# Reworking the first four pairs of an attention-and-MLP kernel, and where pairs 4 to 7 stand

## The chip, the core and the metric

The kernel runs on one core of a Trainium2 chip. The metric is device time in microseconds for one execution. A core has five engines with instruction streams of their own: TensorE (PE; its weight loads are listed as PEld), VectorE (DVE), ScalarE (ACT), GpSimd (POOL) and SyncE (SP). Each works through its stream in order and waits on semaphores. SP here only issues transfers; ACT and POOL issue some of theirs too (in the profile SPq, ACTq, POOLq). Matrix products go to PSUM, which has eight banks of 128 x 512 f32.

## The reference, cut to what matters

```python
# q, k, v: (8, 8, 576, 64), s: (8, 8, 576)
scores = scale * np.matmul(q, k.transpose(0, 1, 3, 2))
s_pos = np.maximum(s, 0.0)
cum = np.cumsum(s_pos, axis=-1)
bias = -(cum[:, :, :, None] - cum[:, :, None, :])
scores = np.where(causal, -1000000000.0, scores + np.minimum(bias, 0.0))
scores = scores - np.max(scores, axis=-1, keepdims=True)
attn = np.exp(scores)
attn = attn / (np.sum(attn, axis=-1, keepdims=True) + 1e-09)
attn_out = np.matmul(attn, v)
x = attn_out.transpose(0, 2, 1, 3).reshape(4608, 512)
h = x @ w_in                          # w_in (512, 2048)
g = h * np.clip(h + 3.0, 0.0, 6.0) / 6.0
out = g @ w_out                       # w_out (2048, 512)
```

## The kernel before, in words

**Units.** There are 64 heads of 576 tokens, handled as 32 pairs. The 4,608 tokens go through the two layers in nine blocks of 512. Four pairs of one batch make up the 512 columns of x for its 576 tokens, so block 0 needs pairs 0 to 3.

**A pair p**, in the order of its tasks:

- `load_qk` (line 136) and `load_v` (146) bring q, k and v from DRAM as f32 through SP's queue, into three buffers in turn (`qkf`, bufs 3, and slot p % 3 of `v_f`). A row of a transfer is the 64 numbers of one token, 256 bytes. Token `t*128 + p` of the pair's 1,152 lies on partition p, column t.
- `load_aug` (159) brings four bias rows per pair, the sums of s split into three f16 parts (`kaug`) and one negated row (`qaug`), from DRAM scratch, where lines 469 and 472 have put them. Together with constant mask rows on partitions 68 to 127 (`mask_rows`, 125, copies from the tile `amask`) they are extra contraction rows of qT and kT, so that the bias comes out of the same product as the scores. For pair 0 the bias rows are copied on the chip (461 to 468).
- `cast_qk` (165) makes q and k f16 on POOL; `cast_v` (226) does it for v, on DVE for pairs 1 to 4 and on POOL otherwise.
- `transpose_group` (242) transposes 128 x 128 tiles on PE with an identity, in two groups (five and four tiles), each into one PSUM bank; DVE copies each group's q and k half to `qT` and `kT` (253).
- `scores_bank` (272) does a head's causal scores in four banks (`BANKS`, 259): products into one of three `S` banks, the exponential on ACT into `Pm` (290), and the triangular mask on POOL (295).
- `attend` (320) multiplies by v with a column of ones, so that the row sums come out too; after the second head of a pair, DVE does reciprocal and product (341, 343) into `xs`. There is one `O` tile of two banks, so the next pair's attend waits for that product.
- `x_transpose` (356) brings `xs` into `xT` through PE and a DVE copy (377), or from pair 8 on by a transposing transfer on SP's queue for three of four pairs. From pair 10 on q and k are transposed by such a transfer too (`cast_columns`, `transpose_dma`), which needs `decay_columns` (179), `load_columns` and `copy_columns` once.

**The layers.** `m1(n, f)` (403) is one of 16 column groups of the first layer of block n: four products of 128 x 512, relu on ACT (416), product on DVE (417) into `gT`. `m2(n, t4, part)` (421) is four products of the second layer; four parts make one 128 x 512 output, which DVE scales (439) and SP stores (441). `load_w_in(h)` and `load_w_out(c)` (382, 388) load the weights on POOL's queue, casting f32 to f16 in the transfer.

**PSUM.** Tag `M` has two banks (`bank`, 53; `half_bank`, 231, for early transposes), `S` three, `O` two, `Y` one.

**The order.** The schedule is written out by hand: what the Python code calls first stands first on each engine. `att_tasks(p)` (482) lists a pair's tasks with costs; `weave` (546) mixes such a list with a list of layer tasks in proportion to the costs, and `merged` (571) mixes the first layer of one block with the second layer of the block before. Before the loop come `keep_warm(18)`, pair 0's cast and transposes and `keep_warm(12)` (584 to 591; products of zeros). Then pairs 0 to 3 and pair 4's scores run alone (592). Block 0's first layer and eight of the sixteen parts of its second layer are woven with the rest of pair 4 and pairs 5 to 8 (602), block 1 with pairs 8 to 12 (603), and so on. In a pair's tasks, the second head of a pair is attended in the pair after it (`late`), and x is transposed there too (`back`).

**Weights.** w_in(0) and w_in(1) are issued by POOL in the tasks of pairs 1 and 2 (479), w_out in four pieces within m1(0) (598).

**Completion semaphores.** The program gives the transfers of SP's and ACT's queues eight semaphores in turn; a transfer waits at its queue's head until the eighth before it is complete.

Of the kernel before, what the change touches and what calls it, by code (L numbers as in the profile page):

```python
# [16 lines left out]
def kernel(  # L17
# [10 lines left out]
    nc = tc.nc  # L28
# [18 lines left out]
    NS = 3  # L47

# [3 lines left out]

    def bank():
        return psum.tile([128, 512], F32, tag="M", bufs=2, name="bank")
# [8 lines left out]
    amask_dram = nc.inline_tensor(amask_np, name="amask")  # L63
# [31 lines left out]
    amask = work.tile([128, 2, SEQ], F16, tag="amask", bufs=1)  # L95
    s_sb = work.tile([NH, SEQ], F32, tag="s0", bufs=1)
    nc.sync.dma_start(out=s_sb, in_=s.rearrange("b h t -> (b h) t"))
    nc.scalar.dma_start(out=amask[64:128], in_=amask_dram.ap().rearrange("i p t -> p i t"))
    nc.scalar.dma_start(out=ident, in_=ident_dram.ap())

# [18 lines left out]
    nc.gpsimd.memset(warm, 0.0)  # L119
    nc.gpsimd.memset(kT[:, :, W2:W2 + 64], 0.0)  # L120
    nc.gpsimd.memset(v_f[64:128, :, :, 4, :], 0.0)
    nc.gpsimd.memset(v_h[:, :, :, :, D:VW], 1.0)
    nc.gpsimd.memset(Pm[:, :, 1600:PW], 1.0)

    def mask_rows(sl, copy):
        for i, dst in enumerate((kT, qT)):
            copy(
                out=dst[64:128, sl, 0:W2].rearrange("p (h t) -> p h t", h=2),
                in_=amask[64:128, i:i + 1, :].to_broadcast([64, 2, SEQ]),
            )  # L130
# [5 lines left out]
    def load_qk(p, eng):  # L136
        b, h0 = (2 * p) // H, (2 * p) % H
        t = work.tile([128, NTR, 2, D], F32, tag="qkf", bufs=3, name=f"qkf{p}")
        for i, src in enumerate((q, k)):
            rows = src[b, h0:h0 + 2].rearrange("h s d -> (h s) d")  # L140
            eng.dma_start(  # L141
                out=t[:, :, i, :], in_=rows.rearrange("(t p) d -> p t d", p=128)
            )
        qk_f[p] = t

    def load_v(p, eng):
        b, h0 = (2 * p) // H, (2 * p) % H
        sl = p % NS
        for hh in range(2):
            eng.dma_start(  # L150
                out=v_f[:, sl, hh, 0:4, :],
# [3 lines left out]
            out=v_f[0:64, sl, :, 4, :],  # L155
# [9 lines left out]
    def cast_qk(p):  # L165
        t = work.tile([128, NTR, 2, D], F16, tag="qkh", bufs=2)
        nc.gpsimd.tensor_copy(out=t, in_=qk_f.pop(p))  # L167
        qk_h[p] = t

    xaug = cpool.tile([128, 2 * NTR, 64], F16, tag="c_xaug")  # L170
# [55 lines left out]
    def cast_v(p):  # L226
        sl = p % NS
        copy = nc.vector.tensor_copy if p in (1, 2, 3, 4) else nc.gpsimd.tensor_copy
        copy(out=v_h[:, sl, :, :, 0:D], in_=v_f[:, sl])  # L229

    def half_bank(early):

        if early:
            return psum.tile([128, 640], F16, tag="M", bufs=2, name="pTm")
# [7 lines left out]
    def transpose_group(p, g):  # L242
        t0, t1 = ((0, 5), (5, 9))[g]
        n = (t1 - t0) * 128
        pT = half_bank(p < 5)
# [10 lines left out]


# [4 lines left out]
        (896, [(1, 256, 576), (4, 512, 576)]),  # L262
# [379 lines left out]
```

## Time and profile before

| | us |
|---|---|
| median of 3 runs | 382.33 (381.08 to 383.68) |
| the profiled execution | 379.86 |
| its span, first to last instruction | 378.1 |
| PE, ACT, DVE, POOL busy in it | 353.6, 210.4, 190.8, 146.4 |
| first scores (L282) | 12.59 |
| first scores of pairs 1, 2, 3, 4 | 16.62, 24.92, 29.86, 36.64 |
| first m1(0) product (L408) | 42.78 |
| first m2(0) product (L430) | 73.16 |
| first m1(1) product | 88.70 |

Times inside the span count from its first instruction. A line of a group gives the source line, engine, operation, output and input tiles, count, then busy time and mean ns. A line of the waits gives who waited for whom, the total, the number and the longest. In a line of stretches the PEclk column is the granted TensorE clock as a share of full speed, and the DMA column the mean busy share of 16 engines, which can exceed 1 where packets of two queues overlap. `q1` is SP's queue, `q10` ACT's and `q0` POOL's.

### The profile page before, as it was taken

How to read it: one execution, taken by the hardware profiler on the slowest of the kernel's cores; microseconds unless marked ns; L12 is line 12 of the kernel's file. 1: busy time of each engine (PE TensorE's matmuls, PEld its weight loads, DVE VectorE, ACT ScalarE, POOL GpSimd, SP SyncE). 2: the span in 40 equal slices, each digit the busy share in tenths (PEclk: the TensorE clock that was granted, in tenths of full speed). 3: DMA queues.
4: the chain of work that ended last, by engine and by line, in shares of the span. 5: the costliest groups of instructions: out<-in, count | busy, mean ns of one | idle time of the engine just before them, and what ended most of it. 6: DMA issues, size and time to landing. Idle time of an engine off the chain costs nothing.

```text
span 378.1 us, 7609 instructions
## 1 busy us (share of the span) xinstructions
PE 353.6 (94%) x2780; PEld 219.8 (58%) x2780; DVE 190.8 (50%) x329; ACT 210.4 (56%) x406; POOL 146.4 (39%) x375
## 2 busy tenths in 40 slices
PE   7766778899999999999999999999999999999995
PEld 3454455566666666666666666666666655555542
DVE  5554466875545444544444445445444554454531
ACT  4745466456866666666656666666666543443310
POOL 4365444364565444444444554454453100000000
PEclk9989699999999999999999999999999999999999
DMA  8699999945999999999999998999854001010011
GB/s 181 137 204 193 194 208 249 210 105 132 200 186 243 204 211 200 216 203 203 197 190 199 214 208 179 206 211 200 185 114 106 31 30 55 28 55 29 28 66 74
DMA packets 184621, 59.38 MB, mean 157 GB/s; under 512 B 177828, under 2 KB 178212, under 8 KB 184584
## 3 DMA queue, kind: packets, MB, share of 16 engines
q1 hardware_dynamic: 182536, 54.52, 68.2%
q0 software_dynamic: 1632, 4.19, 5.9%
q8 instruction: 22, 0.36, 0.4%
q10 hardware_dynamic: 416, 0.19, 0.2%
q14 instruction: 15, 0.12, 0.1%
HBM read 37.41 MB, written 9.73 MB: 125 GB/s over the span
## 4 chain that ended last, share of the span: by engine, by line
PE 82%; DMA 9%; DVE 3%; ACT 2%; SPq 1%; issue 1%; POOL 1%; POOLq 0%; ACTq 0%; DVEq 0%
PE bank L408 31%; PE po L430 30%; PE S L282 9%; PE O L331 7%; DMA qkf<-in_k_dram 5%; DMA v_f<-in_v_dram 3%; PE bank L430 3%; ACT Pm L290 2%; PE pT L369 1%; DMA s_sb<-in_s_dram 1%; PE bank L450 1%; SPq L141 1%; POOL t L167 1%; DVE qkT L253 1%; DVE kaug L115 0%
## 5 line engine op out<-in xcount | busy, mean ns | idle before, releaser
L416 ACT ACTIVATE trl<-bank,bias 128x512 f32<-128x512 f32 x144 | 99.5, 691 | 111.8 <-PE bank L408 110.8
L417 DVE SCALAR_TENSOR_TENSOR gT<-trl,bank 128x512 f16<-128x512 f32 x144 | 99.1, 688 | 121.8 <-ACT trl L416 121.8
L408 PE MATMUL bank<-xT,w_in 128*128 128x512 f16 x576 | 148.3, 383 | 1.3 <-DVE gT L417 1.3
L290 ACT ACTIVATE Pm<-S 128x384 f16<-128x384 f32 (+2 forms) x256 | 116.2, 505 | 32.3 <-PE S L282 30.6
L295 POOL TENSOR_SCALAR_AFFINE_SELECT Pm<-Pm 128x128 f16<-128x128 f16 (+2 forms) x256 | 79.0, 311 | 135.4 <-ACT Pm L290 126.6
L430 PE MATMUL po<-w_out_sb,gT 128*128 128x512 f16 x528 | 130.9, 379 | 0.0
L408 PEld LDWEIGHTS <-w_in 128*128 128x128 f16 x576 | 77.5, 146 | 31.6 <-issue 2.8
L430 PEld LDWEIGHTS <-gT 128*128 128x128 f16 x576 | 53.2, 98 | 51.4
L282 PE MATMUL S<-qkT 128*128 128x320 f16 (+4 forms) x448 | 70.2, 265 | 6.9 <-DVE qkT L253 2.3
L282 PEld LDWEIGHTS <-qkT 128*128 128x128 f16 x448 | 41.4, 99 | 34.2 <-DVE qkT L253 2.7
L331 PEld LDWEIGHTS <-Pm 128*128 128x128 f16 x960 | 39.1, 98 | 12.1 <-POOL Pm L295 0.4
L331 PE MATMUL O<-v_h,Pm 128*128 128x65 f16 x960 | 41.6, 195 | 0.3 <-POOL Pm L295 0.3
L343 DVE TENSOR_TENSOR xs<-O,r 128x640 f16<-128x640 f32 x32 | 26.4, 824 | 1.1
L213 POOL CAST xb<-qkf 128x1152 f16<-128x1152 f32 x22 | 25.3, 1149 | 0.0
L439 DVE TENSOR_SCALAR osb<-po 128x512 f32<-128x512 f32 x33 | 22.6, 685 | 5.0 <-PE po L430 5.0
L229 POOL CAST v_h<-v_f 128x640 f16<-128x640 f32 x28 | 20.6, 737 | 2.2 <-DMA v_f<-in_v_dram 2.2
L341 DVE RECIPROCAL r<-O 128x10 f32<-128x10 f32 x32 | 7.1, 220 | 25.6 <-PE O L331 25.4
L167 POOL CAST t<-qkf 128x1152 f16<-128x1152 f32 x10 | 11.8, 1177 | 12.2 <-DMA qkf<-in_k_dram 12.2
L238 PEld LDWEIGHTS <-t 128*128 128x128 f16 x90 | 6.3, 99 | 12.1 <-POOL t L167 8.2
L253 DVE COPY qkT<-pTm 64x640 f16<-64x640 f16 (+1 forms) x20 | 9.1, 453 | 7.8 <-PE pTm L238 7.6
L450 PE MATMUL bank<-warm 128*128 128x512 f16 x30 | 9.5, 487 | 2.2 <-POOL warm L119 1.4
L430 PE MATMUL bank<-w_out_sb,gT 128*128 128x512 f16 x48 | 11.3, 379 | 0.0
(40 smaller groups left out, 80.2 us busy)
## 6 DMA issues: line engine op xcount, KB each, us to landing
qkf<-in_q_dram SPq DMA_DIRECT2D x32, 288.0 KB, 3.6
qkf<-in_k_dram SPq DMA_DIRECT2D x32, 288.0 KB, 4.2
out_dram<-osb SPq DMA_DIRECT2D x36, 256.0 KB, 2.0
v_f<-in_v_dram SPq DMA_DIRECT2D x64, 128.0 KB, 3.6
w_in<-in_moe_w_in_dram POOLq DMA_DIRECT2D x2, 1024.0 KB, 11.0
w_out_sb<-in_moe_w_out_dram POOLq DMA_DIRECT2D x4, 512.0 KB, 8.3
v_f<-in_v_dram SPq DMA_DIRECT2D x32, 32.0 KB, 8.2
qkT<-xb SPq DMA_TRANSPOSE x22, 5.2
```

Of the source, the lines that this page charges most:

```text
L213: nc.gpsimd.tensor_copy(out=x.rearrange("p (i t) c -> p t i c", i=2)[:, :, :, 0:D], in_=qk_f.pop(p))
L229: copy(out=v_h[:, sl, :, :, 0:D], in_=v_f[:, sl])
L282: nc.tensor.matmul(out=S[:, c:c + hi - lo], lhsT=kT[:, sl, off + 128 * kt:off + 128 * (kt + 1)], rhs=qT[:, sl, off + lo:off + hi], start=( ...
L290: nc.scalar.activation(out=P[:, p0:p0 + n], in_=S[:, 0:n], func=AF.Exp, scale=0.125, bias=0.0)
L295: nc.gpsimd.affine_select(out=view, in_=view, pattern=pattern, compare_op=ALU.is_ge, fill=0.0, base=0, channel_multiplier=-1,)
L331: nc.tensor.matmul(out=O[:, hh, qt * VW:qt * VW + D + 1], lhsT=P[:, c:c + 128], rhs=v_h[:, sl, hh, kt, 0:D + 1], start=(qt == 0), stop=(qt ...
L343: nc.vector.tensor_tensor(out=xs.rearrange("p t h d -> p h t d"), in0=Ov[:, :, :, 0:D], in1=r.to_broadcast([128, 2, 5, D]), op=ALU.mult,)
L408: nc.tensor.matmul(out=ph, lhsT=w_in_t[f // 8][:, kc, f % 8, :], rhs=xT[:, kc, n * 512:(n + 1) * 512], start=(kc == 0), stop=(kc == KC - 1),)
L416: nc.scalar.activation(out=trl, in_=ph, func=AF.Relu, bias=bias3[:, 0:1], scale=1.0)
L417: nc.vector.scalar_tensor_tensor(out=gT[n][:, f, :], in0=trl, scalar=6.0, in1=ph, op0=ALU.min, op1=ALU.mult)
L430: nc.tensor.matmul(out=po, lhsT=gT[n][:, f, t4 * 128:(t4 + 1) * 128], rhs=w_out_sb[:, f, :], start=(f == 0), stop=(f == NF - 1),)
L439: nc.vector.tensor_scalar_mul(out=osb, in0=po, scalar1=1.0 / 6.0)
```

## The change

- **q and k of pairs 0 to 3** are loaded with nine consecutive tokens on a partition, so a row of a transfer is 2,304 bytes. A transposed tile t then holds the tokens `9p + t`.
- **Transposes of those pairs** (`transpose_pair`) put all nine tiles into one two-bank PSUM tile `T`, and `rows_of_head` copies each head's q and k rows out of it in token order, reading every 128th element: four DVE copies of 64 x 576, two of them after the pair's first head.
- **v of pairs 0 and 1** is loaded by POOL's queue, which casts it in the transfer, directly to `v_h`.
- **q and k of pair 0** are cast by ACT, in two halves. A one-column copy to `hold` keeps POOL's cast of pair 1 behind the last `kaug` operation on DVE.
- **Mask rows** of the three slots come by two transfers each from DRAM (ACT's queue for slots 0 and 1, SP's for slot 2); the tile `amask` and the copies on ACT and DVE go.
- **x of a first-batch pair** is transposed two pairs later, into the `Y` bank, and copied by ACT. Pair 3's O is divided head by head.
- **BANKS**: block (4,4) moves to the last bank, so POOL makes three masks a head, not four.
- **Order.** Pairs 0 to 3 run with no layer task. Then `T` is released and `M` opened; m1(0) starts with three of four products for f = 0 to 2 while pair 3 ends, and takes its third bank from `Y`. Pairs 4 and 5 (`pair_with_own`: their own cast, transposes, scores and both attends in one go) are woven with m1(0) from f = 3, pairs 6, 7 and the first tasks of 8 with m2(0); twelve of its parts, not eight, come before block 1.
- **Loads** are re-timed: pair 4 in pair 1, 5 in 3, 6 in 5, 7 and 8 in 6, 9 in 7, 10 and 11 in 8. w_in(0) is issued in pair 1 and w_in(1) after pair 3's scores, w_out from f = 9 on. `keep_warm` is 14 and 14.

The core of the diff:

```diff
+        if p < ROWS:
+                qk_f[p] = t.rearrange("p (i t d) -> p t i d", i=2, t=NTR)
+                eng.dma_start(
+                    out=t[:, i * NTR * D:(i + 1) * NTR * D],
+                    in_=rows.rearrange("(p t) d -> p (t d)", t=NTR),
+                )
...
+        dst = v_h if eng is nc.gpsimd else v_f
...
     def cast_qk(p):
         t = work.tile([128, NTR, 2, D], F16, tag="qkh", bufs=2)
-        nc.gpsimd.tensor_copy(out=t, in_=qk_f.pop(p))
+        if p == 0:
+            for i in range(2):
+                nc.scalar.copy(out=t[:, :, i, :], in_=qk_f[p][:, :, i, :])
+        else:
+            nc.gpsimd.tensor_copy(out=t, in_=qk_f[p])
...
+    load_v(0, nc.gpsimd)
+    load_v(1, nc.gpsimd)
...
-        copy = nc.vector.tensor_copy if p in (1, 2, 3, 4) else nc.gpsimd.tensor_copy
+        copy = nc.vector.tensor_copy if p in (2, 3) else nc.gpsimd.tensor_copy
...
+    def transpose_pair(p):
+        pT = T_tiles[p] = pools["T"].tile([128, 1024], F32, tag="T", name=f"pT{p}").bitcast(F16)
+        src = qk_h.pop(p)
+        for t in range(NTR):
+            transpose_tile(
+                pT[:, t * 128:(t + 1) * 128], src[:, t, :, :], t in (0, 8), t in (7, 8)
+            )
+        rows_of_head(p, 0)
+
+    def rows_of_head(p, hh):
+        pT, sl = T_tiles[p], p % NS
+        for dst, r0 in ((kT, 64), (qT, 0)):
+            nc.vector.tensor_copy(
+                out=dst[0:64, sl, hh * SEQ:(hh + 1) * SEQ].rearrange(
+                    "d (p t) -> d p t", t=NTR
+                ),
+                in_=pT[r0:r0 + 64, 0:W2].rearrange("d (t p) -> d p t", p=128)[
+                    :, hh * 64:(hh + 1) * 64
+                ],
+            )
...
-        (896, [(1, 256, 576), (4, 512, 576)]),
-        (1280, [(2, 256, 576)]),
+        (896, [(1, 256, 576)]),
+        (1216, [(2, 256, 576), (4, 512, 576)]),
...
+        copy = nc.scalar.copy if p < 4 else nc.vector.tensor_copy
+        copy(out=xT[:, hp, b * SEQ:(b + 1) * SEQ], in_=pX[:, 0:SEQ])
...
+    mask_rows(1, nc.scalar)
+    load_qk(2, nc.sync)
     load_aug(1, nc.sync)
+    mask_rows(2, nc.sync)
     load_v(2, nc.sync)
+    load_aug(2, nc.sync)
+    load_qk(3, nc.sync)
+
+    pairs_at = {1: [4], 3: [5], 5: [6], 6: [7, 8], 7: [9], 8: [10, 11]}
...
+    def pair_of_first_batch(p):
+        s0, s1 = scores(2 * p), scores(2 * p + 1)
+        a = [(lambda: loads(p), 0)] + s0[:3]
+        if p > 1:
+            a += xt(p - 2)
+        a += s0[3:]
+        if p < 3:
+            a += [(lambda: transpose_pair(p + 1), 1152)]
+        if p == 0:
+            a += [(lambda: cast_qk(2), 0)]
+        else:
+            a += att(2 * p - 1)
+        if p == 1:
+            a += [(lambda: load_w_in(0), 0)]
+        if p < 3:
+            a += [(lambda: rows_of_head(p + 1, 1), 0)]
+        a += s1
...
+    def pair_with_own(p):
...
+        a = [(own, 0), (lambda: loads(p), 0)] + halves(p)
+        if p < 6:
+            return a + s0 + s1 + att(2 * p) + att(2 * p + 1) + xt(p)
...
+    layers_begin()
+    x_transpose(2)
+    for f in range(2):
+        m1(0, f, range(3))
+    attend(7)
+    m1(0, 2, range(3))
+    x_transpose(3)
+    for f in range(3):
+        m1(0, f, range(3, 4))
...
+    weave(pair_with_own(4), m1_0[3:11])
+    weave(pair_with_own(5), m1_0[11:])
+    for task, _ in m2_0[:2]:
         task()
+    decay_columns()
+    for task, _ in m2_0[2:5]:
+        task()
+    weave(att_of[1], m2_0[5:12])
+    weave(att_of[2], merged(m1_tasks(1), m2_0[12:], 1))
```

## The prediction

> **What bounds the kernel now.** I read the page's busy shares and slices first, then the stretches, PE's waits, the chain, and last the order of instructions on each engine in both programs.
>
> ```profile
> PE 353.6 (94%) x2780; PEld 219.8 (58%) x2780; DVE 190.8 (50%) x329; ACT 210.4 (56%) x406; POOL 146.4 (39%) x375
> PE   7766778899999999999999999999999999999995
> PEclk9989699999999999999999999999999999999999
> ```
>
> PE is the bound from the ninth slice on; only the first 90 us have holes. The busy time by stretch (columns: length, busy PE, PEld, DVE, ACT, POOL with counts, granted clock, DMA share, GB/s):
>
> ```profile
> 0.00:12.60 12.60, 10.04 (x40) 4.04 (x41) 8.46 (x13) 6.36 (x6) 5.23 (x12) 1.00 0.72 144
> 12.60:34.00 21.40, 14.84 (x202) 11.59 (x201) 11.62 (x25) 13.58 (x32) 14.21 (x36) 0.92 0.97 192
> 34.00:49.50 15.50, 9.98 (x70) 6.26 (x68) 5.87 (x11) 6.18 (x12) 6.74 (x15) 0.78 1.03 203
> 49.50:73.20 23.70, 19.38 (x201) 13.66 (x200) 16.73 (x35) 14.33 (x28) 9.39 (x22) 1.00 1.05 222
> 73.20:92.20 19.00, 18.28 (x199) 12.03 (x199) 13.52 (x34) 8.92 (x20) 9.15 (x22) 1.00 0.51 122
> 92.20:300.00 207.80, 207.44 (x1737) 132.46 (x1736) 101.28 (x163) 136.24 (x274) 101.70 (x269) 1.00 0.93 189
> ```
>
> PE idles 2.6+6.6+5.5+4.3+0.7 = 19.7 us up to 92.2 and 0.4 us in the next 208. So the change can win only before 92. What PE waited for there:
>
> ```profile
> PE pTm L238 <- POOL t L167: 4.0, 3, 3.4
> PE S L282 <- DVE qkT L253: 2.3, 2, 1.8
> PE S L282 <- DMA qkT<-kaug_scratch: 2.1, 1, 2.1
> PE pT L238 <- POOL t L167: 1.6, 1, 1.6
> ```
>
> These are late loads: k of pair 2 (3.4), bias rows of pair 4 (2.1), v of pair 4 (1.8, through DVE). The chain has the same names (DMA 9%). Why they are late stands in the DMA view of 36 to 40 us (packets, MB, share), against 16 to 20:
>
> ```profile
> q0 software_dynamic: 366, 0.75, 98.0%
> q1 hardware_dynamic: 316, 0.08, 15.1%
> ```
> ```profile
> q1 hardware_dynamic: 3414, 0.86, 104.8%
> ```
>
> Beside a weight load (q0, 0.98*4*16/366 = 171 ns a packet) SP's queue gets through 79 packets per us, one for each of q0's; alone it does 850. A pair is 3,456 packets of 256 bytes.
>
> **Where the two programs meet.** Before starts m1(1) at 88.70, with 9 of the 16 parts of m2(0) issued; after starts it with 13. A part is 0.863 us (4 of 216 ns), so before stands there at 88.70 + 4*0.863 = 92.15. From there both issue the same PE work, 285.9 us to the end, PE-bound. The sum is the time at which after gets there, minus 92.15. The profiled execution took 379.86 us, 2.47 under the median, 382.33; I add the difference to both.
>
> **Step 1, first scores: 11.4 for 12.59.** DVE's chain from s (landed 3.80) ends at 9.00; its last subtraction took 1.58 beside POOL's cast. `hold` keeps that cast back; L113, the same shape, took 0.75: the chain ends at 8.2 (bounds 8.2 to 9.0). The third bias row is SP's sixth small issue (0.5 to 0.65 each): issued 8.8, landing 2.4 later (L468). PE is at its 14 keep-warm matmuls until 10.9, so q and k (earlier, with ACT's two casts at 0.65) and the strided row copies of head 0 (done by 9.8) are covered. Six v transfers on POOL's queue cost 0.55 to 0.83 each there (rows of the weight issues), under the wait for loads.
>
> **Step 2, pair 1: 15.9 for 16.62.** The bias store goes out 1.9 us earlier, but the load back waits for mask transfers on ACT's queue, which each wait for the completion of the eighth transfer before them: issued 13.9 for 15.21, landing 2.0 later. ACT's exponentials stand behind these issues until 11.6; first scores at 11.4 hide that.
>
> **Step 3, pair 2: 20.8 for 24.92.** Its k is issued at 11.3 for 15.93, and the 3.4 us go. Late next is DVE. `rows_of_head` reads PSUM every 128th element. The nearest rows:
>
> ```profile
> L253 DVE COPY qkT<-pTm 64x640 f16<-64x640 f16 x10 | 4.9, 488 | 7.7 <-PE pTm L238 7.6
> L253 DVE COPY qkT<-pTm 64x512 f16<-64x512 f16 x10 | 4.2, 419 | 0.1
> L205 DVE COPY dec<-pD 128x128 f16<-128x128 f16 x6 | 1.6, 286 | 0.0
> L205 DVE COPY dec<-pD 64x32 f16<-64x32 f16 x6 | 1.1, 184 | 0.0
> ```
>
> Dense 0.54 ns an element; L205, every second element, (286-184)/96 = 1.06. So 64x576 is 0.184+544*0.00106 = 0.76 us if strided, 0.46 if dense (L377); I take 0.76, L205 being the strided row. Per pair 4*0.76 = 3.04 for 1.81. attend(2) needs the O tile, which reciprocal and product (0.22+0.82, L341, L343) release, behind two row copies: transposes end 17.6, +1.52+1.04 = 20.15, +0.6.
>
> **Step 4, pair 3: 28.9 for 29.86.** POOL issues w_in(0) after head 2's third select: exponentials 16.3 to 18.0 (four in 1.7), select 0.4, issue at 18.4 for 26.33. In before the packets began 1.8 after the issue and the first half ran 7.3 us: here 20.2 to 27.5. k of pair 3 is issued at 18.4, v at 19.0 to 21.0, the bias rows at 21.0. k's 128 long packets go one for one with q0: 128*(171+173)/16 = 2.8 us (173: nine small packets of 19.6, an upper bound). k lands at 23.6; cast 1.15, behind which POOL's selects queue; transposes 24.9. v's 1,152 packets and the rows behind them come through after 27.5: +0.7 for the rest, +0.7 to land = 28.9. So 4.1 us won at pair 2 shrink to 1.0. By ACT (1.7 a head, and 0.64 for the x copy it takes over, from L416) the last exponential of head 7 ends at 28.9+0.3+1.7+0.64+1.6 = 33.1, before 33.99.
>
> [...] The 366 against 316 above show one for one, and I go by them.
>
> **Step 5, m1(0) with pairs 4 and 5: 33.1 to 66.0.** PE work: 16 m1 of 0.863 = 13.8; four heads' scores 2.8 and five attends 2.35 (0.70 and 0.47 each, steady state); transposes 1.0, x 1.1: 21.05. Waits, in PE's order, each one the ACT (0.69), DVE (0.69) or POOL work ahead of it: x of pairs 2 and 3 through ACT 1.7; m1 f3 for f0's bank 1.25; first scores of pair 4, whose row copies (0.98) stand behind the relu and product of f5, 2.1; score banks behind relus 0.5; attend(9) for its last select 0.7; x of pair 4 0.85; first scores of pair 5, 2.05; the same four smaller waits again 0.9+0.9+0.8. Sum 11.75; together 32.8. w_in(1), issued at 33.5, is there at 43, before f8 (48).
>
> **Step 6, to m1(1): 66.0 to 94.1.** First m2 parts and decay 6*0.863+1.7 = 6.9. Then 17 us of PE work (9 parts, six heads, five attends, transposes of pairs 6 to 9, x) and 4.2 of waits. The largest is 2.5: loads of pairs 7 and 8 stand on SP behind the first output store, which waits for osb; k of pair 7 is issued at 74, lands 4.2 later, cast 1.15, while PE is ready 2.5 earlier. The rest: row copies ahead of pair 6's and 8's scores, 1.2 and 0.5.
>
> **Sum:** 94.1 - 92.15 = +2.0 us: 379.86 to 381.9 executed, 382.33 to 384.3 median. Costed at nothing, each with its cover:
> - Rows of 2,304 bytes: no step above waits for q or k of pairs 0 to 2, so the time they save has no taker. If k of pair 0 came late after all, the 3 us of keep-warm ahead of the first scores hide it, and beyond that the first scores move one for one.
> - v of pairs 0 and 1 through POOL's queue: issued by 7; even with the 8.3 us that w_out takes to land it is there at 15.3, where attend(0) comes.
> - Masks by six transfers of 144 KB: ACT loses four copies of 1.15, DVE two of 0.87, all in 4.4 to 12.6 beside keep-warm; without that cover they would be worth up to 2 us in step 1.
> - Three selects for four (L295, 0.24 each), cast_v of pair 4 now on POOL (0.72) and that of pairs 2 and 3 still on DVE (0.49): POOL is at 39%, and from 92 on PE is the bound.
> - PSUM: the T tile's two banks become M's when the layers begin; the last T reader is done 3 us earlier.
>
> **Rivals.** *Faster: the block is as dense as before's.* Before's own weave, 49.5 to 73.2, took 23.70 for 19.38 busy, and its first scores waited 0.57 for DVE, not 2.1. At that ratio step 5 is 21.05*23.70/19.38 = 25.7, -7.1: 377.2. For it: the same tasks and one more PSUM bank for m1. Against: attends there belong to the pair before. It holds if first scores of pairs 4 and 5 wait under 0.6.
>
> *Slower: the clock.* In 34 to 49.5 waits of 2.1 and 1.8 went with a granted 0.78. Step 5 idles 11.75 of 32.8. At 0.78 its work takes 27.0, +5.9: 390.2. Against: the clock was 1.00 at 49.5 to 73.2, with smaller waits. It decides if the clock in 33 to 66 is below 0.92.
>
> [...] *The batch gains nothing* (pair 3 at 29.86 again): +1.0, 385.3.
>
> **Chances and range.** My sum 0.32, weights harmless 0.05, batch gains nothing 0.03: within 1% 0.40 (1%, 3.8 us, is about what a measurement of this kernel can tell from no change). Faster 0.27, slower 0.33. Low end: rival one with the weights harmless, 374; high end: the clock rival, 391.
>
> **What would show it.** Right: first scores near 11.4; pair 2's by 21, pair 3's not before 28, waiting for kaug_scratch or POOL's cast beside q0; 2 us holes ahead of the first scores of pairs 4 and 5; a hole ahead of pair 7's transposes. Wrong: pair 3's scores by 26 (step 4), m2(0) starting before 60 (step 5), a clock below 0.92 in the block, strided copies near 0.46, or holes after 94, where SP's issues, back to back at 99 to 115 in before, must serve four pairs in 26 us for 30.

## The result, and the profile after

| | before | changed |
|---|---|---|
| median of 4 runs each, on one chip, us | 382.63 (381.08 to 383.68) | 393.03 (392.22 to 394.11) |
| changed / before, 95% interval | | 1.0277 (1.0229 to 1.0325) |
| span of the profiled execution, us | 378.1 | 390.5 |
| PE's waits between 34 and 104 us | 10.4 | 16.2 |

The change costs 10.4 us, where 2.0 were forecast, and lies above the range's end of 391. The two profiled executions, 379.86 and 392.22 us, are 12.4 apart; all times inside the span come from them. The page of the changed kernel (PE's busy time, its 40 slices, the granted clock):

```profile
PE 355.3 (91%) x2778; PEld 219.4 (56%) x2778; DVE 189.9 (49%) x323; ACT 209.3 (54%) x408; POOL 141.1 (36%) x318
PE   8537776967999999999999999999999999999995
PEclk9997999989999999999999999999999999999999
```

PE has the same work, and it is dense only from the eleventh slice on, for the ninth before. The same stretches as in the prediction, up to the one that was dense before (length, busy PE, PEld, DVE, ACT, POOL, clock, DMA share, GB/s):

```profile
12.60:34.00 21.40, 9.90 (x129) 7.58 (x128) 9.09 (x15) 9.50 (x23) 8.26 (x18) 0.86 0.88 204
34.00:49.50 15.50, 11.59 (x125) 7.98 (x123) 8.81 (x16) 10.15 (x20) 6.12 (x12) 0.98 0.75 140
49.50:73.20 23.70, 17.97 (x161) 11.66 (x161) 13.20 (x25) 13.18 (x26) 10.02 (x20) 1.00 0.65 127
73.20:92.20 19.00, 14.65 (x131) 8.85 (x131) 8.89 (x28) 5.87 (x14) 5.39 (x13) 0.91 0.73 164
92.20:104.00 11.80, 9.37 (x108) 6.27 (x107) 7.18 (x15) 4.44 (x11) 7.42 (x14) 1.00 0.90 208
```

Before, PE worked 14.84, 9.98, 19.38, 18.28 and (from 92.2 on) all of the time. Two stretches lose most: 12.6 to 34 (4.9 us) and 73.2 to 104 (6.1). DMA, over 1.0 before from 34 to 73, now stands at 0.65 to 0.75: transfers no longer fill these stretches, so what PE waited for must be looked up. PE's waits up to 106 us (in total, times, longest):

```profile
PE pT L266 <- POOL t L189: 9.3, 3, 6.3
PE S L334 <- DVE qkT L281: 5.5, 4, 1.9
PE S L334 <- ACT Pm L342: 4.1, 9, 1.1
PE S L334 <- DMA qkT<-qaug_scratch: 2.4, 1, 2.4
```

The 6.3 is pair 3's cast, and a 2.5 in the same row is pair 7's; 1.9 and 1.9 of the second row are the first scores of pairs 4 and 5. The chain that ended last names what is behind the 2.4 and the 6.3 (start, length):

```profile
12.66 4.46 DMA qkT<-amask
17.17 1.40 DMA qkT<-qaug_scratch
21.83 7.99 DMA qkf<-in_k_dram
29.87 1.15 POOL t L189
```

Pair 1's bias rows wait for a mask transfer; k of pair 3 takes 8.0 us from its issue to the cast.

### The profile page after: what moved, and what is told of

Read it like the earlier page. It is cut to its first block, busy times and chain, and to the rows that moved or that the text cites. A ratio compares the mean times of both kernels' runs of the same rounds, so it can differ in the third digit from the quotient of the medians.

```text
span 390.5 us, 7493 instructions
## 1 busy us (share of the span) xinstructions
PE 355.3 (91%) x2778; PEld 219.4 (56%) x2778; DVE 189.9 (49%) x323; ACT 209.3 (54%) x408; POOL 141.1 (36%) x318
## 4 chain that ended last, share of the span: by engine, by line
PE 77%; DMA 8%; ACT 5%; DVE 4%; issue 3%; POOL 2%; SPq 1%; ACTq 0%; POOLq 0%
PE bank L476 29%; PE po L500 28%; PE S L334 9%; PE O L385 6%; ACT Pm L342 3%; DMA qkf<-in_k_dram 3%; PE bank L500 2%; DMA qkT<-xb 1%; DMA qkT<-amask 1%; PE pT L266 1%; DMA qkT<-kaug 1%; ACT trl L486 1%; POOL t L189 1%; DVE gT L487 1%; PE pT L428 1%
## 5 line engine op out<-in xcount | busy, mean ns | idle before, releaser
L487 DVE SCALAR_TENSOR_TENSOR gT<-trl,bank 128x512 f16<-128x512 f32 x139 | 95.5, 688 | 121.6 <-ACT trl L486 121.6
L486 ACT ACTIVATE trl<-bank,bias 128x512 f32<-128x512 f32 x139 | 95.8, 690 | 104.1 <-PE bank L476 102.2
L476 PE MATMUL bank<-xT,w_in 128*128 128x512 f16 x556 | 142.4, 381 | 2.1 <-DVE gT L487 1.1
L347 POOL TENSOR_SCALAR_AFFINE_SELECT Pm<-Pm 128x256 f16<-128x256 f16 (+1 forms) x192 | 70.8, 373 | 155.2 <-ACT Pm L342 150.8
L385 PEld LDWEIGHTS <-Pm 128*128 128x128 f16 x960 | 37.8, 98 | 13.3 <-POOL Pm L347 2.0
L400 DVE TENSOR_TENSOR xs<-O,r 128x640 f16<-128x640 f32 (+1 forms) x33 | 26.5, 804 | 1.1
L399 DVE RECIPROCAL r<-O 128x10 f32<-128x10 f32 (+1 forms) x33 | 7.2, 217 | 28.5 <-PE O L385 28.5
L300 DVE COPY qkT<-pT 64x576 f16<-64x576 f16 x16 | 12.1, 754 | 13.3 <-PE pT L266 12.9
L266 PE MATMUL pT<-ident,t 128*128 128x128 f16 x90 | 7.9, 235 | 10.3 <-POOL t L189 9.3
L281 DVE COPY qkT<-pT 64x640 f16<-64x640 f16 (+1 forms) x24 | 10.9, 454 | 10.4 <-PE pT L266 10.1
L189 POOL CAST t<-qkf 128x1152 f16<-128x1152 f32 x9 | 10.3, 1150 | 11.2 <-DMA qkf<-in_k_dram 11.2
```

The lines of the kernel that those rows point to most:

```text
L347: nc.gpsimd.affine_select(out=view, in_=view, pattern=pattern, compare_op=ALU.is_ge, fill=0.0, base=0, channel_multiplier=-1,)
L385: nc.tensor.matmul(out=O[:, hh, qt * VW:qt * VW + D + 1], lhsT=P[:, c:c + 128], rhs=v_h[:, sl, hh, kt, 0:D + 1], start=(qt == 0), stop=(qt ...
L400: nc.vector.tensor_tensor(out=x_tiles[p].rearrange("p t h d -> p h t d")[:, h0:hh + 1], in0=Ov[:, :, :, 0:D], in1=r.to_broadcast([128, hh ...
L476: nc.tensor.matmul(out=ph, lhsT=w_in_t[f // 8][:, kc, f % 8, :], rhs=xT[:, kc, n * 512:(n + 1) * 512], start=(kc == 0), stop=(kc == KC - 1),)
L486: nc.scalar.activation(out=trl, in_=ph, func=AF.Relu, bias=bias3[:, 0:1], scale=1.0)
L487: nc.vector.scalar_tensor_tensor(out=gT[n][:, f, :], in0=trl, scalar=6.0, in1=ph, op0=ALU.min, op1=ALU.mult)
```

## The experiments

My theory after the result: the time is lost to single late things, each of them movable: loads (k of pair 3 starved beside w_in(0), bias rows behind masks, pair 7 behind the output store) and work that stands right ahead of its user (row copies of pairs 4 and 5). The rival: the spread order is slow by itself, with too little other PE work beside a pair, and a wait taken away comes back elsewhere. Ratios are to the kernel before, run on the same chip.

### Single mends on the changed kernel

**The weights later.**

```diff
-        if p == 1:
-            a += [(lambda: load_w_in(0), 0)]
...
-            a += [(lambda: cast_qk(3), 0)]
+            a += [(lambda: cast_qk(3), 0), (lambda: load_w_in(0), 0)]
```

> The changed kernel with one task moved: the first half of w_in is issued on POOL's queue behind the cast of pair 3's q and k, in place of ahead of head 3's scores. Theory (pair 3's loads starve beside the weight packets): pair 3's k lands at about 25, 2 us after its issue, PE's 6.3 us wait for POOL's cast falls under 2, and pair 3's first scores come at about 29 (bias rows issued at 26.3 land by 28.8) for 32.84; the half itself is there at about 36, where m1 begins, so some of it is given back: 387.5 to 391 us. Rival (k of pair 3 is late because of where it stands in SP's order; the weights only stand beside it): the wait stays above 5 us and the time is 393 or more.

Measured: 1.022 (1.0116 to 1.0323); its four times spread over 388.2 to 395.5 us, and the profiled execution took 394.88, so the total settles nothing. The trace bears the theory out on k: k of pair 3 was issued at 22.03 for 21.83 and was there at 25.2 for 29.9; the 6.28 wait fell to 0.69. The new wait is the weights' own:

```profile
38.00 2.78 PE L476 MATMUL bank<-xT,w_in 128*128 128x512 f16 x6 [3.67 <-DMA w_in<-in_moe_w_in_dram]
```

Six matmuls in 2.78 us, where four took 1.02 in the changed kernel: in this execution the granted clock was 0.68 from 34 to 49.5.

**k of pair 3 first.**

```diff
     load_qk(2, nc.sync)
+    load_qk(3, nc.sync)
     load_aug(1, nc.sync)
...
     load_aug(2, nc.sync)
-    load_qk(3, nc.sync)
```

> The changed kernel with q and k of pair 3 issued right behind those of pair 2 (at about 12.7 us), ahead of pair 1's bias rows; the weight load stays where it is. Both theories have the 6.3 us wait go. Theory (starving beside the weights): the next to be late are the bias rows of pair 3, which stand behind 1,152 packets of v of pair 3 beside the weights until these end at about 30.3: scores of pair 3 at 31 to 32 for 32.84, so the time is 391 to 392.5 us, and PE waits 2 us or more for kaug_scratch or qaug_scratch there. Rival (order of issue alone): nothing else is late, scores of pair 3 at about 29, 388 to 390 us.

Measured: 389.47 us, 1.0187 (1.0134 to 1.0239), a time where the rival had it. Pair 3's first scores came at 31.73, where the theory had them, but the expectation took its base wrongly: 32.84 is head 5, head 6 stood at 35.27. So 3.5 us are won, all of them kept up to m2(0) (67.58 for 71.12). The bias rows were late by 0.54 only, not by 2 or more; next was attend(4)'s wait for the O tile, 1.0.

**Transposes of pairs 4 and 5 earlier.**

```diff
+    h4, h5 = pair_with_own(4), pair_with_own(5)
+    for task, _ in h4[0]:
+        task()
-    weave(pair_with_own(4), m1_0[3:11])
-    weave(pair_with_own(5), m1_0[11:])
+    weave(h4[1] + h4[2] + h4[3] + h5[0] + h4[4], m1_0[3:11])
+    weave(h5[1] + h5[2] + h5[3] + h5[4], m1_0[11:])
```

A pair's list comes in five parts here: casts, loads and transposes; scores of the two heads; first attend; second attend and x.

> The changed kernel with the transposes and row copies of pairs 4 and 5 one step earlier: those of pair 4 ahead of m1 f3, those of pair 5 between the two attends of pair 4 (their loads and casts with them). Theory (the two waits of 1.90 us ahead of the first scores of pairs 4 and 5 are DVE's order alone): both fall under 0.5 us, block 0 gets 3 to 4 us shorter, 388.5 to 390.5 us. Rival (DVE's copies ahead of the products of f3 to f5 only move the wait to m1's banks and to the later casts of v): a gain under 1 us, 392 to 393.

Measured: 389.66 us, 1.0193 (1.0130 to 1.0256). Both waits of 1.90 went, and two others came: pair 5's cast stands behind pair 4's selects on POOL, and pair 5's row copies ahead of pair 4's product on DVE:

```profile
55.91 0.45 PE L266 MATMUL pT<-ident,t 128*128 128x128 f16 x5 [1.58 <-POOL t L189]
60.62 0.45 PE L428 MATMUL pT<-ident,xs 128*128 128x128 f16 x5 [1.79 <-DVE xs L400]
```

From m1 f0 to m2(0) the block took 30.0 us for 31.8; the clock of 73 to 92 was 1.00 for 0.91, by my estimate 1.7 us more (0.09 of 19 us), though the wait ahead of pair 7's transposes was there as before (2.50 for 2.55), so that this part is the edit's is not shown. Theory and rival each hold for half.

**Masks without overlap.**

```diff
+                r0 = 3 + i
+                eng.dma_start(out=dst[64 + r0:128, sl, 0:W2], in_=amask_dram.ap()[i, r0:])
+    nc.gpsimd.memset(qT[64:67, 1:NS, 0:W2], 1.0)
```

(for slots 1 and 2; slot 0 as it was)

> The changed kernel with the mask transfers of slots 1 and 2 cut so that they no longer write the rows that the bias rows write (three rows for k, four for q; the three constant rows of q by one memset on POOL): pair 1's and 2's bias rows then overwrite nothing and need not wait for the mask transfers. Theory (the wait of 3.1 us on SP behind the masks of slot 1 sets pair 1's scores, and pushes all later issues on SP): pair 1's bias rows are issued at about 13, its first scores come at about 16.5 for 18.70, q and k of pair 3 are issued at about 18.5 for 21.4, ahead of the weights, and the 6.3 us wait shrinks by 3 or more: 386 to 389.5 us. Rival (the mask transfers' bytes and their completions in turn hold SP whatever they write): first scores of pair 1 stay at 18 or later, 392 to 393 us.

Measured: 396.32 us, 1.0364 (1.0308 to 1.0420): slower, for another reason than either. Pair 1's rows were issued at 13.49 for 15.79, as the theory has it, but the masks themselves landed only at 25. DMA from 17 to 25 us (packets, MB, share of 16 engines), and PE's wait:

```profile
q1 hardware_dynamic: 50, 0.11, 3.4%
q10 hardware_dynamic: 44, 0.10, 3.1%
```
```profile
25.19 1.53 PE L339 MATMUL S<-qkT 128*128 128x256 f16 x7 [9.38 <-DMA qkT<-amask]
```

94 packets in 8 us, 6.5% of 16 engines, as much as the whole time of one (0.065 x 16 = 1.04). The transfers now have 61 and 60 rows; SP's of 60 rows landed 13.3 us after its issue, where with 64 rows they landed in 2.8 to 4.3 us. Why they took so much longer, and what 61 or 60 rows do by themselves, no run shows.

**Masks first.**

```diff
     mask_rows(0, nc.scalar)
+    mask_rows(1, nc.scalar)
...
     load_qk(1, nc.sync)
+    mask_rows(2, nc.sync)
```

(and their old places emptied)

> The changed kernel with the mask transfers of slots 1 and 2, whole as they were, issued among the first: slot 1's on ACT behind slot 0's, slot 2's on SP behind q and k of pair 1. Theory (pair 1's bias rows wait for the masks that they overwrite, and everything behind them on SP is late with them): the rows are issued at about 13.5 as in the run with the masks cut apart, pair 1's first scores come at about 16.2 for 18.70, k of pair 3 is issued by 18 and lands ahead of the weights, the 6.3 us wait shrinks by 3 or more: 386.5 to 389.5 us. Rival (288 KB twice more in the first 6 us make q and k of pair 0 late): the first scores move from 12.0 to 13.5 or later, and the gain is under 1.5 us.

Measured: 387.71 us, 1.0193 (1.0132 to 1.0254). Both had part of it. Pair 0's bias rows came behind the masks: first scores at 15.78 for 12.03, and pair 1's at 20.28 for 18.70. Yet the ratio fell from 1.0277 to 1.0193, some 3 us: POOL, later now too, issued w_in(0) at 22.94, behind k of pair 3 (21.37) and not ahead of it, and the 6.28 wait was 0.71. The rows were issued 3.12 us behind the kaug store (17.68 for 14.56), as without overlap (13.49 for 10.40, 3.09): the store is the floor, and in the changed kernel (15.79 for 10.72) the masks add 2.0 to it.

**Pair 7 early, then its cast early as well.**

```diff
+    loads(6)
     for task, _ in m2_0[:2]:
```
```diff
+        if p == 6:
+            a += [(lambda: cast_qk(7), 0)]
```

(the second edit in the second run only, with own(7) rid of this cast)

> The changed kernel with the loads of pairs 7 and 8 issued ahead of the first parts of m2(0), so that they no longer stand on SP behind the first output store. Theory (this store holds them): k of pair 7 is issued at about 70 for 79.8, the 2.55 us wait ahead of its transposes goes, and with it the stretch at a granted 0.91 (73 to 92 us), 1.7 us: 388 to 390.5 us. Rival (w_out's packets hold them as they hold v of pair 6 up to 68, or the hole only moves to the next late thing): over 1.5 us of the wait is there again and the time is 392 or more.

> The run with the loads of pairs 7 and 8 early, and the cast of pair 7's q and k ahead of pair 6's selects on POOL. In the run without this, k of pair 7 had landed by 75, and its cast began at 84.68, right behind the last select of head 13 (84.33). Theory (the 2.55 us wait is POOL's order, not the load): it falls under 0.5, the granted clock of 73 to 92 stays 1.00, 388 to 390.5 us. Rival (something behind it, selects or row copies, is late next by as much): 391 us or more.

Measured: 392.23 us, 1.0306 (1.0243 to 1.0368), and 388.91 us, 1.0173 (1.0145 to 1.0201). In the first, k was issued at 71.89 for 79.77 and the wait was still 2.25. POOL in that run:

```profile
84.33 0.41 POOL L347 TENSOR_SCALAR_AFFINE_SELECT Pm<-Pm 128x256 f16<-128x256 f16 x1 [0.42 <-ACT Pm L342]
84.68 1.14 POOL L189 CAST t<-qkf 128x1152 f16<-128x1152 f32 x1
```

The cast has no wait of its own: it starts when head 13's last select ends, and that select waits for exponentials. With the cast ahead of those selects the wait was gone; the clock was 1.00 through 73 to 92 in both runs. So two things held the cast to nearly the same time in the changed kernel: POOL's order, which by itself kept 2.25 of the 2.55 us, and the late load (cast at 84.47, 0.24 behind POOL). The run that took the wait away had moved both; the cast alone was not moved.

### The two halves of the change apart

**The first batch alone, ahead of the order of before.**

```diff
+    for task, _ in halves(4) + att_of[0]:
+        task()
+    first = [(task, 0.0 if f < 4 else 0.7) for f, (task, _) in enumerate(m1_tasks(0))]
...
+    weave(att_of[1], first + m2_0[:8])
+    weave(att_of[2], merged(m1_tasks(1), m2_0[8:], 2))
```

(`att_of` from pair 4 on, and the loads from there, as in the kernel before)

> One part of the change alone: the first batch of the changed kernel (rows, v, transposes, masks, pairs 0 to 3), and behind it the order of the kernel before: pair 4 ahead of the layers, pairs 5 to 8 woven through m1(0) and the first half of m2(0), m1(1) merged in two rounds. Theory (the first batch gains about nothing with its late loads, and the loss of 10 us is the spread order with its waits): m1 f0 starts at 42 to 44 (42.78 before), 381 to 385 us. Rival (the late loads of the first batch cost it all, the new order costs nothing): 389 us or more.

Measured: 380.51 us, 1.0010 (0.9974 to 1.0046). Level with before, and by the ratios 10 us under the changed kernel, with the same late loads (pair 3 still waited 5.5). Its stretches:

```profile
49.50:73.20 23.70, 20.86 (x203) 14.84 (x202) 18.39 (x35) 16.23 (x31) 10.71 (x20) 1.00 1.01 207
73.20:92.20 19.00, 18.42 (x211) 12.34 (x208) 13.70 (x37) 8.55 (x19) 8.61 (x18) 1.00 0.52 126
```

m1 f0 started only at 46.68 (42.78 before), so of the expected 42 to 44 nothing came; what it lost there this order caught up by m1(1) (89.07 for 88.70). All of the 10 us thus comes with the spread of pairs 4 to 7. It is not the waits of that spread alone, though: here a first batch that was 3.9 us late was made up by m1(1), while in the spread order k first, a mend of the batch, won 3.5 us. The order of before hides a late batch, the spread order does not.

**The spread order with its work a step ahead.** Casts of pair p+1 at the start of pair p, its transposes between p's two heads, loads one pair earlier:

```diff
+        tr = halves(p + 1)
+        a += [(lambda: cast_qk(p + 1), 0)] + s0 + tr[:1]
+        b = s1 + [(lambda: cast_v(p + 1), 0)] + tr[1:]
...
+    pairs_at = {1: [4], 3: [5], 4: [6], 5: [7], 6: [8], 7: [9], 8: [10, 11]}
```

> The spread order itself with what a pair needs done a step ahead: casts of pair p+1 at the start of pair p on POOL, its transposes and row copies between the two heads' scores of pair p (pair 4's behind m1 f2), loads of pairs 6 to 8 one pair earlier and ahead of the first output store. The first batch with its late loads stays. Theory (the spread order lost its 10 us to waits right behind what feeds them): PE's waits between 34 and 104, 16.2 us in the changed kernel and 6.7 in the batch alone, fall to 9 or less, 384 to 388 us. Rival (the waits are the spread order's own, because PE has too little other work beside a pair there, and only change their names): 13 us or more of waits, 389 us or more.

Measured: 383.11 us, 1.0008 (0.9987 to 1.0029), a little under the theory's range. PE's waits between 34 and 104 fell from 16.2 to 8.7; the largest that are left:

```profile
PE S L334 <- ACT Pm L342: 2.6, 6, 0.6
PE pT L428 <- DVE xs L400: 2.3, 2, 1.1
PE bank L476 <- ACT xT L437: 1.0, 2, 0.7
```

In these 70 us no wait for a cast or a row copy is over 0.8 any more. The batch's late loads are all still there, and the 10 us are back. The rival falls: the spread order is not slow by itself, its work stood in the wrong places.

**Mends of the batch ahead of the order of before.** k of pair 3 first in all three; masks first in the first, masks copied (the edit is shown below) in the others; in the third pair 7's loads one pair earlier:

```diff
     load_qk(2, nc.sync)
+    load_qk(3, nc.sync)
...
-    pairs_at = {1: [4], 3: [5], 4: [6], 5: [7, 8]}
+    pairs_at = {1: [4], 3: [5], 4: [6, 7], 5: [8]}
```

> The kernel of the run with the batch alone, with the two mends of its loads: q and k of pair 3 behind those of pair 2, and the masks of slots 1 and 2 among the first. Theory (the gains of the two add up and reach the order of before, whose PE is dense): m1 f0 starts 4 to 6 us earlier than in the batch alone, 376 to 380 us, faster than both kernels. Rival (the time won is lost again waiting for the weights or for pair 5's loads beside them): less than 1.5 us under the batch alone.

> The batch alone ahead of the order of the kernel before, with the two mends that gave 377.9 us in the spread order: masks of slots 1 and 2 copied, q and k of pair 3 right behind those of pair 2. Theory (the order of before is bound near 65 us by transfers, which in it come in the same order whatever the first batch gains): m1 f0 starts 4 us or more earlier than in the batch alone (46.7), but the transposes near 65 us wait 1.5 us or more for POOL's cast and the time stays at 379 to 381.5 us, above the spread order with the same mends. Rival (the earlier mended batch lost its gain to the masks that stood ahead of its first bias rows): 376 to 378.5 us, as fast as the spread order or faster.

> The batch alone with both mends, ahead of the order of before, and the loads of pair 7 one pair earlier, with those of pair 6. In seven traces so far k of pair 7 lands at 64 where it is issued behind the first piece of w_out (before, 3.7 us behind; the mended batches), and in time where it is issued 0.3 us ahead (the batch alone). Theory (the old order's bound at 65 us is that order of two issues, which an earlier batch turns round): k of pair 7 is issued by 43, ahead of w_out (46), the 4.2 us wait at 65 goes, and the batch's gain stays: 375 to 377.5 us. Rival (the transfers are full up to 65 us, so something else is late by as much): a wait of 1.5 us or more at 60 to 70 again, 379 us or more.

The first two took 381.13 us, 0.9996 (0.9962 to 1.0030), and 379.36 us, 0.9922 (0.9879 to 0.9965); the second one's profiled execution took 382.44. m1 f0 came at 44.53 and 41.80 for 46.68, and in both executions PE waited near 65 us for POOL's cast of pair 7 (1.78 and 4.20 us). By the ratios the first run kept next to nothing of its gain, the second 3.4 us under the batch alone. That cast in the kernel before, and in the first of the two:

```profile
63.99 1.15 POOL L167 CAST t<-qkf 128x1152 f16<-128x1152 f32 x1 [2.85 <-DMA qkf<-in_k_dram]
```
```profile
64.04 1.15 POOL L190 CAST t<-qkf 128x1152 f16<-128x1152 f32 x1 [2.77 <-DMA qkf<-in_k_dram]
```

| | w_out's first piece issued | k of pair 7 issued | its cast begins |
|---|---|---|---|
| before | 46.14 | 49.85 | 63.99, waits for k |
| batch alone | 47.94 | 47.68 | 63.44, no wait for k |
| mended, masks first | 45.79 | 53.91 | 64.04, waits for k |
| mended, masks copied | 46.23 | 49.91 | 64.44, waits for k |
| the same, pair 7 early | 44.32 | 49.52 | 61.60, waits for scores |
| masks copied, misplaced (last part) | 46.87 | 46.58 | 61.88, no wait for k |
| misplaced, k of pair 3 first | 48.57 | 48.28 | 64.34, waits for k |

w_out is tied to m1(0), so a batch that is done earlier sends it out ahead of pair 7's loads. That this order decides when k is there, as I expected, the table does not bear out: issued 0.3 us ahead of w_out, k still took 16.1 us to its cast in the last row, and the cast waited for it:

```profile
64.34 1.15 POOL L201 CAST t<-qkf 128x1152 f16<-128x1152 f32 x1 [0.25 <-DMA qkf<-in_k_dram]
```

Issued 5.2 us behind w_out, in the run with pair 7 early, it was there within 12.1 us. That run took 377.27 us, 0.9865 (0.9817 to 0.9913): the wait of 4.20 us (in the execution of 382.44) is 1.23, and there, by the profile, POOL waited for scores and not for k:

```profile
61.60 1.15 POOL L201 CAST t<-qkf 128x1152 f16<-128x1152 f32 x1 [2.21 <-PE S L346]
```

By its own numbers (a wait of 1.5 us or more, 379 us or more) the rival falls. The theory is not shown either. Its condition was not met: k went out at 49.5, behind w_out, since v of pair 6 held SP's queue from 39.1 to 46.9, and yet it was there by 61.6. The gain over the run without this edit (0.9922) is not clear of noise, the intervals overlap. What sets when k of pair 7 arrives is open.

### The best of both

**k of pair 3 first, masks copied, both, and short rows, on the spread order with its work ahead.** Masks copied:

```diff
-    mask_rows(1, nc.scalar)
+    mask_copy(1, nc.scalar.copy)
...
+    mask_copy(2, nc.vector.tensor_copy)
```

(from one transfer of 144 KB into `amask`, as in the kernel before; slot 2's behind `rows_of_head(0, 1)` and ahead of `load_aug(2)`.)

Short rows: `ROWS = 0`, and `rows_of_head` copies 576 consecutive columns.

> The spread order with its work a step ahead, and q and k of pair 3 issued right behind those of pair 2. Theory (in this order each late load still costs its wait, and the order has no other bound before 100 us): pair 3's 5.1 us wait goes, as it did in the changed kernel, 3 to 4 us: 379 to 380.5 us, faster than both kernels. Rival (as in the mended batch ahead of the old order, something at 65 us, a load beside the weights, takes it all back): 382 us or more.

> The spread order with its work a step ahead, and the masks of slots 1 and 2 copied on the chip from one transfer of 144 KB: slot 1's by ACT where its transfers were issued, slot 2's by DVE behind pair 0's row copies and ahead of pair 2's bias rows. Theory (pair 1's rows wait for the masks that they overwrite): pair 1's rows are issued by 14, its first scores come by 16.5 for 18.4, SP's later issues move up by 2 or more, so k of pair 3 is ahead of the weights and the 5.1 us wait shrinks to 2 or less: 378 to 381 us. Rival (the rows wait for their own store and transfers, or the copies hold ACT or DVE as long): first scores of pair 1 at 17.8 or later, 382 us or more.

> Both: masks copied, and q and k of pair 3 right behind those of pair 2. Theory (the masks alone already bring k of pair 3 ahead of the weights): within 1 us of the run with the masks copied, 377.5 to 381 us. Rival (k of pair 3 is late for its order, whatever the masks do): 2 to 4 us less than that run.

> The spread order with its work a step ahead, but q and k of pairs 0 to 3 in rows of 256 bytes as in the kernel before, and so with dense row copies (0.46 us estimated for 0.75). Theory (long rows pass beside the weights, short ones go one for one with 171 ns packets): k of pair 3 lands later, its wait grows from 5.1 to 7 us or more, 385 to 388 us. Rival (my prediction's: no step waits for q or k of pairs 0 to 2, and the dense copies give DVE 1.2 us a pair): 382 to 383.5 us.

| | us | ratio to before (95%) | w_in(0) issued | k of pair 3 issued | its cast begins |
|---|---|---|---|---|---|
| work ahead | 383.11 | 1.0008 (0.9987 to 1.0029) | 20.84 | 21.56 | 28.66 |
| + k first | 379.29 | 0.9896 (0.9864 to 0.9928) | 21.98 | 13.53 | 24.87 |
| + masks copied | 378.34 | 0.9863 (0.9831 to 0.9896) | 23.59 | 20.57 | 25.83 |
| + both | 377.88 | 0.9851 (0.9818 to 0.9884) | 22.69 | 14.53 | 24.99 |
| work ahead, short rows | 385.22 | 1.0046 (1.0003 to 1.0089) | 24.00 | 23.61 | 33.74 |

In this order a load's wait is worth what it lasts: k first brings some 4 us, as in the changed kernel. The masks copied bring as much, yet not in the way that the theory said: pair 1's first scores came at 20.89, later than 18.37, since ACT's copies end at 16.87 and the exponentials stand behind them (a wait of 2.98). What they changed for pair 3 is again the order of two issues: k now goes out 3 us ahead of the weights, and its cast does not wait for it. So both together add only 0.5. With both, the kernel takes 1.5% less than before and, by the ratios, some 16 us less than the changed one. The old order with pair 7 early does the same (0.9865): with these mends the two orders are level. PE's slices in the run with both:

```profile
PE   6587778989999999999999999999999999999996
```

Short rows are not settled by time: five of their twelve runs took 381.3 to 382.2 us, seven 385.1 to 386.9. In the profiled one (386.83 us) k of pair 3 went out 0.4 us ahead of the weights and still took 10.1 us to the cast, where long rows 1.6 us ahead (masks first) took 4.7. This execution was late from the start: pair 0's transposes came at 9.79 for 7.77, SP had issued pair 0's small bias rows by 14.9 for 9.8, and the first scores came at 17.17 for 11.90.

**Masks copied ahead of the order of before, misplaced.** In these two the copy of slot 2's masks stands behind pair 2's bias rows and overwrites them, so heads 4 and 5 get no bias of theirs, and DVE's queue stands until the rows have landed (PE waited 4.21 and 4.78 us for row copies ahead of pair 1's scores).

```diff
     load_aug(2, nc.sync)
...
+    mask_copy(2, nc.vector.tensor_copy)
```

> The batch alone, with the masks of slots 1 and 2 copied on the chip again, as in the kernel before, from one transfer of 144 KB (slot 1 by ACT ahead of its casts, slot 2 by DVE behind pair 0's row copies); slot 0's stay transfers. Theory (the four transfers, 576 KB, hold pair 1's rows and take 2 us of a DMA system that is full up to 65 us): pair 1's first scores at about 16 for 18.5, all later loads 2 us or more earlier, 376.5 to 379 us. Rival (what is won early is waited for again at pair 3's k and at 65, where the weights set the time): 379.5 us or more.

> The same with q and k of pair 3 issued right behind those of pair 2. Theory (each of the late loads costs its wait): another 2 to 4 us, 373.5 to 377 us. Rival (as in the mended batch, a wait for a cast near 65, 1.78 us, and a half clock behind it give all of it back): within 1 us of the run before it.

Measured: 379.76 us, 0.9916 (0.9886 to 0.9946), and 380.15 us, 0.9945 (0.9924 to 0.9966). Both are under the batch alone in spite of a hole of 4 us in the first batch, and k first added nothing. In both, k of pair 7 was issued 0.3 us ahead of w_out, and PE had no wait for its cast near 65 us, though in the second the cast itself waited for k (the table above).

## Why the prediction was wrong, point by point

It met m1(1) at 94.1; the changed kernel was there at 103.47, 9.4 later (6.2 at m1 f0, 5.1 at m2(0)), and lost 1.1 more between 104 and 130 (PE busy 24.89 of 26.0). With the 2.0 that were forecast this is about the 12.4 us between the two profiled executions; the medians are 10.4 apart. The terms that failed are in steps 2, 4 and 6:

- **Step 1** (first scores 11.4): 12.03, the last bias row landing 0.45 late. Right in kind, 0.6 short: DVE's chain began 0.37 later (s landed at 4.17) and ended at 8.60, its last subtraction in 0.75 as forecast.
- **Step 2** (pair 1 at 15.9): 18.70, the first term that was mis-sized. I had the rows wait for mask transfers at 13.9; they were issued at 15.79 and 17.17. They overwrite rows that the masks write, so they wait for the landing (12.66 + 4.46 in the chain). That is +2.2 at pair 1, and SP's queue stands behind them: k of pair 3 went out at 21.83 for 18.4. Shown by the run without overlap (issue at 13.49).
- **Step 3** (pair 2 at 20.8): 23.49, all of the difference carried over. The strided copy was right: 754 ns in 16 of 16 for 0.76.
- **Step 4** (pair 3 at 28.9): 35.27, +3.7 beyond what it brought along. The culprit was right, the size and the last wait were not: k of pair 3 was to share one for one with the weights and take 5.2 us, landing at 23.6; it took 8.0 and landed at 29.8. So its cast ended last, and not the bias rows, which I had last at 28.9: behind pair 3's transposes (31.07) PE still had two attends and head 5's scores ahead of 35.27, and with k first the rows were late by 0.54 only. DMA in the changed kernel from 24 to 26 us:

```profile
q0 software_dynamic: 189, 0.39, 106.7%
q1 hardware_dynamic: 9, 0.01, 2.8%
```

  Nine of SP's packets to 189, then 85 to 147 and 229 to 158 in the next two pairs of us. I took 366 to 316 from the middle of a weight load in the kernel before; here SP's queue got almost nothing at first, so that number could not be used. (Nine packets of 19.6 ns are 176, not 173; the 2.8 us stays.) Why SP's queue stands still at first is open.
- **Step 5** (32.8 us from m1 f0 to m2(0)): 31.8. The waits of 1.90 and 1.90 ahead of pairs 4 and 5 were forecast as 2.1 and 2.05, the attends' 0.37 and 0.41 as 0.7. The best of the steps: the spread order waited as forecast. A mend of its waits and of step 6's brings 10 us back, but they were in the sum; the forecast did not fail here.
- **Step 6** (28.1 us): 32.35. Its waits sum to 6.8 for 4.2 and the clock of 0.91 over 19 us took, by the estimate above, 1.7 that I had at nothing. The 2.5 ahead of pair 7 had the right size and one of two causes: I named the output store on SP; with the store out of the way 2.25 were left, and the cast ahead of six selects as well took them away.
- **Costed at nothing.** Masks by transfers were not: through step 2 they also decide whether k of pair 3 goes out ahead of the weights. Rows of 2,304 bytes may have a taker: with short rows the first scores came at 17.17 for 11.90 in the one execution profiled, but the twelve times do not settle it. v on POOL's queue and PSUM left no wait; the selects left the two of step 5 that were forecast.
- **Rivals.** *Faster, a dense block* needs the work a step ahead, which the change has not. *The clock* stood at 0.98 and 1.00 from 34 to 73, where I had set it, and fell to 0.91 from 73 to 92. Its 390.2 us is the nearest of my numbers to the measured 393.03, by luck, for its reason was not met. *Weights harmless*: no run shows the 3.2 us that the range's low end of 374 takes off 377.2 for it; beside the weights k of pair 3 took 8.0 us to its cast, and PE waited 6.28. *The batch gains nothing* had pair 3 at 29.86; it came at 35.27, and the batch alone is level with before since the order of before made up 3.9 us.

The range added one unknown at a time, and steps 1, 2, 4 and 6 missed on the same side. A first batch that came late (steps 2 and 4) met an order that does not hide it; step 6's waits and clock came on top, for reasons of their own.

## What to carry to other kernels

When a load shares the system with a long weight load, ask which of the two is issued first: here k of pair 3 took 8.0 us issued 0.65 us behind, 4.7 issued 1.6 us ahead and 3.2 with the weights moved away, and whatever moved either queue (masks, a cast, a select) turned the order round. It is no rule: for w_out and pair 7 the order of issue did not tell when k was there. When a wait names a cast or copy, look at what stands ahead of it on that engine before looking at its load. And do part of the change by itself: the first batch alone was level, the spread was the loss, and the batch's mends brought the time under that of before only with the work behind it moved ahead, or in the order of before.

## What the runs showed of the hardware that was not expected

- Transfers of 61 and 60 rows on two queues went at 94 packets in 8 us, 6.5% of 16 engines' time, and SP's of 60 rows landed 13.3 us after its issue; 64 rows took 2.8 to 4.3.
- From 24 to 26 us, just after a weight load had begun to stream, SP's queue got 9 packets for its 189; from 28 to 30 us 229 for 158.
- With rows of 256 bytes, issued 0.4 us ahead of the weights, the 288 KB of k took 10.1 us; with rows of 2,304 bytes, issued 1.6 us ahead, 4.7, in one profiled execution each. How much of this is the rows and how much the place is not shown.
- Single waits of PE of 2.55 us (changed kernel) and 2.58 us (k first) ahead of pair 7's transposes went with a granted clock of 0.91 from 73 to 92 us; waits of 2.25 us (pair 7 early) and 2.50 us (transposes early) at the same place went with 1.00.
